# Chunk 0's second products on half rows, with the two PSUM banks exchanged between the halves

## The chip, the cores and the metric

The kernel runs on one core of one Trainium2 chip. Times are device microseconds of one execution; lower is better. Besides the timed runs there is one profiled execution, whose trace is read here. In the trace PE is the tensor engine (its matmuls; PEld its weight loads), DVE the vector engine, ACT ScalarE, POOL GpSimd, and SP the engine that issues most DMAs.

## The reference

`x` is (4, 4096, 192), `weight_gen` (4, 4096, 8, 7), `w_in` (192, 2048), `w_out` (2048, 192).

```
w = softmax(weight_gen, axis=-1)                 # 7 taps for each of 8 heads
att[b,s,h,:] = sum_k w[b,s,h,k] * x[b, s-6+k, h*24:(h+1)*24]    # zeros before the start
h = att.reshape(16384, 192) @ w_in               # float64 weights in memory
g = max(0.01 * h, h)
out = g @ w_out                                  # (16384, 192) float32
```

## The kernel before, in words

**Tiling.** The 16384 tokens are 32 chunks of 512 (`NCH`, `TOK`). The 2048 inner features are 16 blocks of 128 (`NF`), taken two at a time in 8 steps a chunk (`NQ`). Step q of the whole run belongs to chunk q // 8. In each step `mm1` computes `hp[2q]` and `hp[2q+1]` (128 features x 512 tokens each, one PSUM bank each): the first products. It works on half rows: the 192 inputs are three pairs of 64, and of every pair of matmuls one uses the upper and one the lower 64 rows of the array (`HALVES`), so the two run side by side. ScalarE applies the leaky ReLU, and the second products (`g` times a block of `w_out`) are summed over the 16 blocks in PSUM.

**Chunks 1 to 31** use f16 numbers split in an upper and a lower part (`wi_h`, `wi_l`, `g_h`, `g_l`). Their second products too use half rows: in one pass the upper rows write one bank and the lower rows another, and in a later pass they exchange. Two row groups must not write one bank at a time, so a nop on SP (`tell`, line 626) waits for the last matmul before the exchange, and the first one after it waits for the nop.

**Chunk 0** uses f32, because the scales of the f16 split are not known yet: the weights' maxima are being collected while chunk 0 is computed. An f32 matmul shows as two records in the trace, each streaming its columns twice. Its second products are in `mm2_whole` (line 649): for each block n four matmuls of 128 x 128 by 192 columns, on all 128 rows, into two banks `po0[0]` and `po0[1]`, each holding two row blocks of 128 tokens. `evacuate_whole` (line 662) copies `po0[0]` out on ScalarE and `po0[1]` on VectorE; the sums of chunk 1 (`new_sums`) take the same banks afterwards, and the first pair of `mm2_first` writes both.

**Order.** Each engine runs its instructions in the order written. The order of the first part is the string `START` (lines 55 to 62), one letter an action: `r` ScalarE reads a weight block's two words (`rnd`, then `mag`; lines 140, 141), `W` VectorE widens and adds them into `bits` (lines 151, 156), `m` takes the block's maximum (line 184), `f` is a step of first products with its two leaks on ScalarE, `e` is `mm2_whole` for one block, `p` and `q` are steps of the next chunks' convolution on GpSimd, `T` (`first_tokens`, line 419) copies the transposed tokens of chunk 0 from PSUM. `1`, `2`, `3` are the chain of the scales: two transposes of `both` on the PE (line 214), a matmul with `ones` (line 222), then the powers of two on VectorE (lines 191 to 228). `v`, `h`, `l` scale a block and split it into halves (VectorE line 241, ScalarE 249, VectorE 253); `H` and `L` (lines 258, 264) do the same without the copy in PSUM. `M N E B D C V y Y X R` prepare chunk 1's tokens.

The weight blocks come in the order of `order` (lines 722 to 725), (q, IN) for the first and (q, OUT) for the second products; the DMAs on SP, the reads and all later stages follow it. Tiles `rnd` and `mag` have three buffers each, `hp` four banks, `g` six.

From step 8 on `step(q)` (line 795) writes the order: first products, leak and cast of each `hp` (lines 567, 582) with VectorE's subtraction for `g_l` (line 585), the second products. In step 8 (`WHOLE * NQ`) it runs `mm2_whole` for the last two blocks of chunk 0 (`HOLD`) and `evacuate_whole`; `mm2_first` of chunk 1 starts in step 10. In chunk 1 every step also converts one weight block (`HL`) until all are done.

Of the kernel before, what the change touches and what calls it, by code (L numbers as in the profile page):

```python
# [8 lines left out]
F32 = mybir.dt.float32  # L9
F32R = mybir.dt.float32r  # L10
U32 = mybir.dt.uint32
I32 = mybir.dt.int32
F16 = mybir.dt.float16
AF = mybir.ActivationFunctionType
ALU = mybir.AluOpType
# [22 lines left out]

WHOLE = 1

HOLD = 2

TURNS = {1: (2, 3)}

G0 = 20
# [7 lines left out]
HEAT = 11  # L53

START = (
    "ZASgdgdtgdtgdrtgdtagdtgdWrttbT"
    "Wprmf"
    "WmrprfpWmrWpmrf"
    "WpmrWmreeeeWpmrWmrWpmrf"
    "WmrpsfWmrpWmreeeeWmrppppMNEBDCVWmfWmmf"  # L60
    "ee1yYXe2e3RvvhhllevvhhllevvhhllfvvhhllqqHL"
)


# [1 line left out]
def conv_attention_moe_kernel(  # L66
# [66 lines left out]
    NW = NB * P  # L133
    vals = {}

    def read_words(key):
        w = words.pop(key).rearrange("p a b w -> p (a b) w")
        rnd = raw.tile([P, NW], U32, tag="rnd", name="rnd", bufs=3)
        mag = raw.tile([P, NW], F32, tag="mag", name="mag", bufs=3)
        nc.scalar.activation(out=rnd, in_=w[:, :, 0], func=AF.Copy, scale=2.0 ** -29)  # L140
        nc.scalar.activation(  # L141
            out=mag, in_=w[:, :, 1].bitcast(F32), func=AF.Prelu, scale=REBIAS, alpha=SIGN
        )
        vals[key] = rnd, mag.bitcast(U32)

    def widen(key, add=False):

# [27 lines left out]
    most = const.tile([P, 2, NQ], F32, name="most")  # L175
    both = const.tile([P, 2], F32, name="both")
    scale = const.tile([P, 2, 2], I32, name="scale")[:, :, 0]
    back = const.tile([P, 2, 2], I32, name="back")[:, :, 0]
    undo = const.tile([P, 1], F32, name="undo")
    ones = const.tile([1, P], F32, name="ones")  # L180

# [26 lines left out]
    def weight_scales(i):  # L208

        if i == 0:  # L210
            nc.vector.tensor_reduce(out=both, in_=most, axis=AX.X, op=ALU.max)
            chain["t"] = spare()
            for k in range(2):
                nc.tensor.transpose(
                    out=chain["t"][0:1, k * P:(k + 1) * P], in_=both[:, k:k + 1], identity=ident
                )
        elif i == 1:
            row = chain.pop("t")[0:1, 0:2 * P].rearrange("p (k t) -> p k t", k=2)
            top = const.tile([1, 2], F32, name="top")
            nc.vector.tensor_reduce(out=top, in_=row, axis=AX.X, op=ALU.max)  # L220
            chain["b"] = spare()
            nc.tensor.matmul(out=chain["b"][:, 0:2], lhsT=ones, rhs=top, start=True, stop=True)  # L222
        else:
            e = spare()[:, 0:2].bitcast(I32)
            exponents(chain.pop("b")[:, 0:2], e)
            powers(e, scale, back)
            b = back.bitcast(F32)
            nc.vector.tensor_scalar(
                out=undo, in0=b[:, 0:1], scalar1=b[:, 1:2], scalar2=1.0 / DOWN,
                op0=ALU.mult, op1=ALU.mult,  # L230
            )

    def scale_of(key):
        return scale.bitcast(F32)[:, key[1]:key[1] + 1]
# [181 lines left out]
                skip_group_check=True,  # L416
            )

    def first_tokens():

        new_xx(0)
        lo, hi = HALVES
        x = xx[0].rearrange("p k i b t -> p (k i b t)").rearrange("p (n t) -> p n t", t=2 * P)
        a, b, c = (t[:, 0:2 * P] for t in sums)
        act, dve = nc.scalar.copy, nc.vector.tensor_copy
        act(out=x[:, 1], in_=a)  # L428
        dve(x[:, 2], b)
        softmax_exp(0, SECOND)  # L430
        act(out=x[:, 5], in_=c)
        dve(x[lo, 3], b[hi])
        act(out=x[lo, 0], in_=a[hi])
        dve(x[hi, 4], b[lo])
        act(out=x[hi, 0], in_=a[lo])
        dve(x[hi, 3], c[lo])
        act(out=x[lo, 4], in_=c[hi])

    def first_rows(b):

# [4 lines left out]

    FIRSTS = (
        (0, 0, 0), (1, 1, 0), (0, 2, 0), (1, 0, 1), (0, 1, 1), (1, 2, 1),
        (0, 1, 0), (1, 0, 0), (0, 0, 1), (1, 2, 0), (1, 1, 1), (0, 2, 1),
    )

    def mm1_first():
# [194 lines left out]
        for n in ns:  # L646
            del g_h[n], g_l[n]

    def mm2_whole(ns):

        for n in ns:
            f = n % NF
            for j in range(J):
                nc.tensor.matmul(  # L654
                    out=po0[j // 2][:, j % 2 * D:(j % 2 + 1) * D],
                    lhsT=g_h[n][:, POS[j] * P:(POS[j] + 1) * P], rhs=value((f // 2, OUT))[:, f % 2],
                    start=(f == 0 and j % 2 == 0), stop=(f == NF - 1 and j % 2 == 1),
                    skip_group_check=True,
                )
            del g_h[n]  # L660

    def evacuate_whole(c):

# [55 lines left out]
                    eng = nc.sync  # L719
                eng.dma_start(out=out_rows[:, r + j, :], in_=ot)  # L720

    order = [(0, IN), (1, IN), (2, IN), (0, OUT)]
    for q in range(3, NQ):
        order += [(q, IN), (q - 2, OUT)]
    order += [(NQ - 2, OUT), (NQ - 1, OUT)]
    done = dict.fromkeys("rwomvhl", 0)
    stages = dict(
# [22 lines left out]
    with tc.manual_schedule():  # L750
# [27 lines left out]
                else:  # L778
                    n -= 1

        pending = []

        def firsts(q):

# [10 lines left out]
        def step(q):  # L795

            c, i = divmod(q, NQ)
            if i == 0 and c in sm_q:
                load_weights(sm_q[c])
                load_rows(sm_q[c])  # L800
            if i == 1 and c in sm_q:
                softmax_max(sm_q[c])
                softmax_sub(sm_q[c], nc.gpsimd)
            begun, told = pending.pop() if pending else (None, None)
            mm1(q)
            leak(2 * q)
            if begun:
                mm2_second(begun, told)
                if begun[-1] % NF == NF - 1:
                    evacuate(begun[-1] // NF)  # L810
            if q == NP - 1:
                leak(2 * q + 1)
                split_g(2 * q, nc.vector)
            else:
                split_g(2 * q)
                if c + 1 < NCH and i == TURNS.get(c, (1, 3))[1] + 1:
                    squares(c + 1, 1)
                leak(2 * q + 1)
            split_g(2 * q + 1)
            if q == WHOLE * NQ:  # L820
                mm2_whole(range(2 * q - HOLD, 2 * q))
                evacuate_whole(c - 1)
            elif firsts(q):
                ns = firsts(q)
                pending.append((ns, tell(mm2_first(ns))))
            if c == WHOLE:
                for what in "HL":
                    if done[what.lower()] < len(order):
                        prepare(what)
            if i == 0:  # L830
                feed(c + 1, 2 * K)
            if c + 1 < NCH:
                first, turned = TURNS.get(c, (1, 3))
                if i == first:
                    scale_tokens(c + 1)
                if i == first + 1:
                    split_h(c + 1)
                    split_l(c + 1, nc.gpsimd)
                if i == turned:
                    squares(c + 1, 0)  # L840
                if i == turned + 1:
                    put_squares(c + 1)
                if i == turned + 2:
                    get_squares(c + 1)
                if i >= first:
                    feed(c + 2, 1 if c == WHOLE and i == first else 3)
            finish_softmax(c, i)
# [24 lines left out]
                    out=t, lhsT=zeros[:, 0:P], rhs=zeros, start=True, stop=True  # L872
                )

        n, added, ended = 0, 0, 0
        for what in START.replace(" ", ""):
            if what in stages:
                prepare(what)
# [31 lines left out]
                add_transposed(added)  # L910
                added += 1
            elif what == "T":
                first_tokens()
            elif what in "123":
                weight_scales("123".index(what))
            elif what == "B":
                scale_tokens(1)
            elif what == "M":
                softmax_max(1)
            elif what == "N":  # L920
                softmax_sub(1, nc.gpsimd)
            elif what == "E":
                softmax_exp(1)
            elif what == "D":
                m = spare()[:, 0:R * H].unsqueeze(2)
                sm[1] = win.tile([P, R * H, 1], F32, tag="sm", name="sm")
                nc.vector.tensor_reduce(out=m, in_=grouped(1, ALL), axis=AX.X, op=ALU.add)
                nc.vector.tensor_scalar_add(out=m, in0=m, scalar1=1e-9)
                nc.vector.reciprocal(out=sm[1], in_=m)
                softmax_div(1, nc.gpsimd)  # L930
            elif what == "q":
                feed(2, 1)
            elif what == "C":
                split_h(1)
            elif what == "V":
                split_l(1, nc.gpsimd)
            elif what in "yY":
                squares(1, "yY".index(what))
            elif what == "X":
                put_squares(1)  # L940
            elif what == "R":
                get_squares(1)
            elif what == "f":
                mm1(n) if n else mm1_first()
                leak_out(2 * n)
                leak_out(2 * n + 1)
                n += 1
            elif what == "e":
                mm2_whole([ended])
                ended += 1  # L950
            else:
                raise ValueError(what)
        for n in range(n, NP):
# [36 lines left out]
```

## Time and profile before

| what | value |
|---|---|
| median of 3 runs | 1029.55 us (1029.2 to 1030.83) |
| profiled execution | 1029.38 us, span 1027.6 us |
| PE busy | 1021.4 us, 99% of the span |
| ACT busy | 661.9 us, 64% |
| DVE busy | 570.8 us, 56% |
| POOL busy | 802.6 us, 78% |
| chunk 0's second products (line 654) | 128 records, 22.3 us of matmuls |
| chunk 0's first products (lines 458, 561) | 108 records in f32 |

The span is the time from the first to the last instruction; the execution's own time is 1.78 us longer. Busy shares are means over stages with different limits; the change is in the first 62 us.

### The profile page before, as it was taken

How to read it: one execution, taken by the hardware profiler on the slowest of the kernel's cores; microseconds unless marked ns; L12 is line 12 of the kernel's file. 1: busy time of each engine (PE TensorE's matmuls, PEld its weight loads, DVE VectorE, ACT ScalarE, POOL GpSimd, SP SyncE). 2: the span in 40 equal slices, each digit the busy share in tenths (PEclk: the TensorE clock that was granted, in tenths of full speed). 3: DMA queues.
4: the chain of work that ended last, by engine and by line, in shares of the span. 5: the costliest groups of instructions: out<-in, count | busy, mean ns of one | idle time of the engine just before them, and what ended most of it. 6: DMA issues, size and time to landing. Idle time of an engine off the chain costs nothing.

```text
span 1027.6 us, 30264 instructions
## 1 busy us (share of the span) xinstructions
PE 1021.4 (99%) x12821; PEld 906.9 (88%) x12821; DVE 570.8 (56%) x1033; ACT 661.9 (64%) x1264; POOL 802.6 (78%) x514
## 2 busy tenths in 40 slices
PE   8999999999999999999999999999999999999998
PEld 7778888988889898898988999899998988989897
DVE  8996545554545555455555455545456554555443
ACT  6586666666657666666666666666566666666664
POOL 7989798777897777887777987778987779987600
PEclk9999999999999999999999999999999999999999
DMA  9521312303232132322213123032321323120120
GB/s 256 166 91 48 126 48 71 117 28 116 63 110 64 44 99 63 118 55 63 95 48 126 48 65 119 26 122 63 97 78 40 103 63 115 58 64 33 48 63 17
DMA packets 42662, 83.08 MB, mean 81 GB/s; under 512 B 4511, under 2 KB 36127, under 8 KB 40734
## 3 DMA queue, kind: packets, MB, share of 16 engines
q1 hardware_dynamic: 42382, 81.05, 25.9%
q8 instruction: 100, 1.64, 0.7%
q14 instruction: 36, 0.29, 0.1%
q10 hardware_dynamic: 144, 0.10, 0.0%
HBM read 56.36 MB, written 24.77 MB: 79 GB/s over the span
## 4 chain that ended last, share of the span: by engine, by line
PE 99%; DMA 1%; SPq 0%; DVE 0%; ACT 0%; issue 0%; ACTq 0%
PE hp L561 52%; PE po L614 44%; PE po L654 2%; DMA wi_raw<-in_moe_w_in_dram 0%; PE hp L458 0%; DMA wt<-in_weight_gen_dram 0%; SPq L127 0%; SPq L283 0%; ACT mag L141 0%; DVE oe L715 0%; DVE wt L318 0%; ACT rnd L140 0%; DVE mx L315 0%; PE spares L222 0%; ACT xw L428 0%
## 5 line engine op out<-in xcount | busy, mean ns | idle before, releaser
L585 DVE TENSOR_TENSOR gl<-hp,gh 128x512 f16<-128x512 f32 x496 | 338.2, 688 | 379.8 <-ACT gh L582 376.3
L614 PE MATMUL po<-wo,gh 64*128 64x384 f16 (+1 forms) x4096 | 539.4, 318 | 0.0
L614 PE MATMUL po<-wo,gl 64*128 64x192 f16 x3968 | 519.6, 243 | 0.0
L561 PE MATMUL hp<-xx,wi_h 64*128 64x512 f16 x2976 | 501.7, 376 | 0.0
L567 ACT ACTIVATE hp<-hp 128x512 f32<-128x512 f32 x496 | 292.3, 589 | 269.9 <-PE hp L561 269.9
L614 PEld LDWEIGHTS <-gh 64*128 64x128 f16 x4096 | 375.7, 94 | 12.5
L561 PE MATMUL hp<-xx,wi_l 64*128 64x512 f16 x1488 | 381.5, 376 | 0.0
L614 PEld LDWEIGHTS <-gl 64*128 64x128 f16 x3968 | 369.0, 94 | 10.2 <-DVE gl L585 0.2
L363 POOL TENSOR_TENSOR acc<-acc,tmp 128x768 f32<-128x768 f32 x186 | 336.7, 1810 | 14.6
L582 ACT CAST gh<-hp 128x512 f16<-128x512 f32 x495 | 290.7, 587 | 16.1 <-PE po L614 1.5
L359 POOL TENSOR_TENSOR tmp<-xt,wt 128x768 f32<-128x768 f32 x186 | 287.7, 1547 | 10.0
L561 PEld LDWEIGHTS <-wi_h 64*128 64x128 f16 x2976 | 255.4, 94 | 45.4 <-issue 1.1
L561 PEld LDWEIGHTS <-wi_l 64*128 64x128 f16 x1488 | 139.3, 94 | 33.1
L502 POOL TENSOR_TENSOR acc<-acc,xu 128x768 f32<-128x768 f32 x30 | 44.1, 1470 | 137.7 <-DVE xu L201 137.7
L697 DVE SCALAR_TENSOR_TENSOR ot<-po,xr,ot 128x192 f32<-128x192 f32 x120 | 41.7, 410 | 50.6 <-ACT ot L693 50.6
L521 DVE STREAM_TRANSPOSE sq<-split 128x384 f16<-128x384 f16 x124 | 63.9, 554 | 8.7 <-POOL split L512 8.2
L508 ACT CAST split<-acc 128x768 f16<-128x768 f32 x31 | 25.8, 832 | 51.1 <-POOL acc L502 48.9
L512 POOL TENSOR_TENSOR split<-acc,split 128x768 f16<-128x768 f32 x31 | 50.9, 1643 | 1.0 <-ACT split L508 0.9
L359 POOL TENSOR_TENSOR acc<-xt,wt 128x768 f32<-128x768 f32 x31 | 48.1, 1553 | 1.2 <-ACT wt L323 1.2
L693 ACT ACTIVATE ot<-po,xr 128x192 f32<-128x192 f32 x120 | 40.7, 422 | 0.7
L485 DVE TENSOR_REDUCE xm<-acc 128x4 f32<-128x768 f32 x30 | 28.3, 943 | 0.3 <-POOL acc L363 0.3
L654 PEld LDWEIGHTS po<-bits,g 128*128 128x128 f32 x128 | 20.6, 190 | 2.7 <-DVE bits L156 1.5
(94 smaller groups left out, 291.6 us busy)
## 6 DMA issues: line engine op xcount, KB each, us to landing
xx<-far SPq DMA_DIRECT2D x124, 192.0 KB, 3.8
xt<-in_x_dram SPq DMA_DIRECT2D x14, 1344.0 KB, 5.7
far<-sq SPq DMA_DIRECT2D x31, 384.0 KB, 2.3
out_dram<-ot SPq DMA_DIRECT2D x62, 192.0 KB, 1.9
wt<-in_weight_gen_dram SPq DMA_DIRECT2D x15, 224.0 KB, 2.5
wi_raw<-in_moe_w_in_dram SPq DMA_DIRECT2D x16, 192.0 KB, 6.5
wo_raw<-in_moe_w_out_dram SPq DMA_DIRECT2D x8, 384.0 KB, 8.4
xt<-in_x_dram SPq DMA_DIRECT2D x2, 384.0 KB, 4.0
```

Source lines behind the costliest of these rows:

```text
L359: eng.tensor_tensor(out=out, in0=tap(c, k), in1=wk, op=ALU.mult)
L363: eng.tensor_tensor(out=acc, in0=acc, in1=out, op=ALU.add)
L502: nc.gpsimd.tensor_tensor(out=att[c], in0=att[c], in1=up.bitcast(F32).to_broadcast([P, J, D]), op=ALU.mult)
L512: eng.tensor_tensor(out=l, in0=att.pop(c), in1=h, op=ALU.subtract)
L521: nc.vector.transpose(out=sq[c][:, v, i], in_=src[:, v])
L561: nc.tensor.matmul(out=hp[2 * q + u], lhsT=w[s], rhs=r[u], start=(m == 0), stop=(m == len(passes) - 1),)
L567: return nc.scalar.activation(out=hp[n], in_=hp[n], func=AF.Prelu, alpha=0.01, scale=DOWN).ins
L582: nc.scalar.copy(out=h, in_=t)
L585: nc.vector.tensor_tensor(out=l, in0=t, in1=h, op=ALU.subtract)
L614: ins = nc.tensor.matmul(out=po[j][:, 0:b - a], lhsT=g[n][s, j * P:(j + 1) * P], rhs=wo[s, f, a:b], start=(f == 0 and i < HALF and m == 0) ...
L654: nc.tensor.matmul(out=po0[j // 2][:, j % 2 * D:(j % 2 + 1) * D], lhsT=g_h[n][:, POS[j] * P:(POS[j] + 1) * P], rhs=value((f // 2, OUT))[:, ...
L697: nc.vector.scalar_tensor_tensor(out=ot[:, j], in0=po[k * HALF + j][:, 0:D], scalar=rx[j], in1=ot[:, j], op0=ALU.mult, op1=ALU.add,)
```

## The change

Chunk 0's second products go from `mm2_whole` to `whole_rows`: each block's products on the upper 64 rows of the array go into one bank and those on the lower 64 rows into the other, side by side; `(` is this first half for one block. `|` (`turn_rows`) puts a nop on ScalarE that waits for the last such matmul, and exchanges the banks; `)` is the second half, whose first matmul waits for the nop. In most steps the PE now does `))((` and then `f`. The last two blocks' second halves and the copies out of `po0` move from step 8 to step 9, and step 8 gets the weight instructions `hhllHL` instead, which no longer stand in `START`.

A second-products block now stands one place sooner in `order`. In `first_tokens` the read of the second weight block no longer stands ahead of the copies but between them, and the matmuls of the first step are reordered to the copies. The scales' inverse goes to PSUM first; `undo` is computed later (`u`).

```diff
-    "ZASgdgdtgdtgdrtgdtagdtgdWrttbT"
+    "ZASgdgdtgdtgdrtgdtagdtgdWttbT"
     "Wprmf"
-    "WmrprfpWmrWpmrf"
-    "WpmrWmreeeeWpmrWmrWpmrf"
-    "WmrpsfWmrpWmreeeeWmrppppMNEBDCVWmfWmmf"
-    "ee1yYXe2e3RvvhhllevvhhllevvhhllfvvhhllqqHL"
+    "Wrpmf"
+    "((WrpmWrmr|f"
+    "))((WprmWrmrWpmr|f"
+    "))((WpmrWpmrWmr|f"
+    "))((spWmrWrmWmpppppM|NEfBDCV"
+    "))((WmWmm|f"
+    "))((1((yYX2|3vvhhlluRf"
+    "))))((vvhhllvvhhllqqvv|"
...
-            powers(e, scale, back)
...
+            chain["d"] = spares[0][:, NW:NW + 2].bitcast(I32)
+            powers(e, scale, chain["d"])
...
         softmax_exp(0, SECOND)
+        read_rnd(key)
+        dve(x[lo, 3], b[hi])
         act(out=x[:, 5], in_=c)
-        dve(x[lo, 3], b[hi])
+        dve(x[hi, 4], b[lo])
+        read_mag(key)
         act(out=x[lo, 0], in_=a[hi])
-        dve(x[hi, 4], b[lo])
-        act(out=x[hi, 0], in_=a[lo])
         dve(x[hi, 3], c[lo])
         act(out=x[lo, 4], in_=c[hi])
+        act(out=x[hi, 0], in_=a[lo])
...
+    def turn_rows():
+
+        told = nc.scalar.nop().ins
+        tc.add_manual_dep(told, last[0].name, after, reason="rows to leave")
+        gate.append(told)
+        turned[0] ^= 1
+
+    def whole_rows(n):
+
+        f = n % NF
+        for i in range(HALF):
+            for u, s in enumerate(HALVES):
+                k = u ^ turned[0]
+                ins = nc.tensor.matmul(
+                    out=po0[k][:, i * D:(i + 1) * D],
+                    lhsT=g_h[n][s, POS[k * HALF + i] * P:(POS[k * HALF + i] + 1) * P],
+                    rhs=value((f // 2, OUT))[s, f % 2],
...
+                if gate:
+                    tc.add_manual_dep(ins, gate.pop().name, after, reason="rows left")
+        last[0] = ins
...
-    order = [(0, IN), (1, IN), (2, IN), (0, OUT)]
-    for q in range(3, NQ):
-        order += [(q, IN), (q - 2, OUT)]
+    order = [(0, IN), (1, IN)]
+    for q in range(2, NQ):
+        order += [(q - 2, OUT), (q, IN)]
...
             if q == WHOLE * NQ:
-                mm2_whole(range(2 * q - HOLD, 2 * q))
+                for what in "hhllHL":
+                    prepare(what)
+            elif q == WHOLE * NQ + 1:
+                for n in range(ended[0], NF):
+                    whole_second(n)
                 evacuate_whole(c - 1)
```

## Rows read from the trace of the kernel before

**Rows 1.** The page: engines' busy time, and the clock in 40 slices.

```profile
PE 1021.4 (99%) x12821; PEld 906.9 (88%) x12821; DVE 570.8 (56%) x1033; ACT 661.9 (64%) x1264; POOL 802.6 (78%) x514
...
PEclk9999999999999999999999999999999999999999
```

**Rows 2.** The chain of waits in order of time: start us, us, what ran.

```profile
19.84 5.40 PE po L654 x32
25.24 5.35 PE hp L561 x24
...
41.34 2.80 PE po L654 x16
...
50.06 4.72 PE hp L561 x30
54.78 2.80 PE po L654 x16
```

**Rows 3.** Timeline of PE, narrow windows: start, us, instruction, records merged.

```profile
17.50 1.05 PE L561 MATMUL hp<-xw,bits 64*128 64x512 f32 x4
18.79 1.05 PE L561 MATMUL hp<-xw,bits 64*128 64x512 f32 x4
20.04 0.49 PE L654 MATMUL po<-bits,g 128*128 128x192 f32 x2
24.91 0.33 PE L654 MATMUL po<-bits,g 128*128 128x192 f32 x1
...
43.97 0.38 PE L214 MATMUL spares<-ident,both 128*1 128x128 f32 x2
44.19 1.47 PE L654 MATMUL po<-bits,g 128*128 128x192 f32 x8
...
61.41 0.32 PE L614 MATMUL po<-wo,gh 64*128 64x384 f16 x1
```

**Rows 4.** Weight loads by form: count, busy us, mean ns, idle before.

```profile
L654 PEld LDWEIGHTS po<-bits,g 128*128 128x128 f32 x128 | 20.6, 190 | 2.7 <-DVE bits L156 1.5 <-DVE spares L151 0.8 <-ACT g L572 0.4
L561 PEld LDWEIGHTS hp<-xw,bits 64*128 64x128 f32 x84 | 8.2, 187 | 8.4 <-issue 8.4
```

**Rows 5.** Timelines of PE and ACT where the first products start.

```profile
10.44 0.60 PE L412 MATMUL ta<-ident,parts 128*128 128x128 f32 x4
11.80 2.89 PE L458 MATMUL hp<-xw,bits 64*128 64x256 f32 x24 [0.55 <-ACT xw L428]
...
11.39 0.36 ACT L428 COPY xw<-ta 128x256 f32<-128x256 f32 x1
```

**Rows 6.** Timeline of ACT: the reads numbered 10 and 11.

```profile
24.49 0.56 ACT L140 ACTIVATE rnd<-wo_raw 128x384 uint32<-128x384 uint32 x1 [1.34 <-DVE most L184]
...
26.09 0.56 ACT L140 ACTIVATE rnd<-wi_raw 128x384 uint32<-128x384 uint32 x1 [0.59 <-DVE most L184]
26.56 0.54 ACT L141 ACTIVATE mag<-wi_raw 128x384 f32<-128x384 f32 x1
27.68 0.56 ACT L140 ACTIVATE rnd<-wo_raw 128x384 uint32<-128x384 uint32 x1 [0.57 <-DMA wo_raw<-in_moe_w_out_dram]
```

**Rows 7.** Timeline of ACT in steps 8 and 9.

```profile
55.13 0.48 ACT L249 CAST wi_h<-spares 128x384 f16<-128x384 f32 x1 [0.16 <-DVE spares L241]
...
56.03 0.62 ACT L258 ACTIVATE wi_h<-bits,scale 128x384 f16<-128x384 f32 x1
56.55 0.59 ACT L567 ACTIVATE hp<-hp 128x512 f32<-128x512 f32 x1
...
58.76 0.48 ACT L671 COPY ot<-po 128x384 f32<-128x384 f32 x1
```

**Rows 8.** Timeline of DVE in step 8.

```profile
58.89 0.69 DVE L585 TENSOR_TENSOR gl<-hp,gh 128x512 f16<-128x512 f32 x1 [0.41 <-ACT gh L582]
59.50 0.55 DVE L669 COPY ot<-po 128x384 f32<-128x384 f32 x1
```

**Rows 9.** Line 264 (`L`): count, ns min/median/max, first and last start.

```profile
L264 DVE SCALAR_TENSOR_TENSOR wo<-bits,scale,wo x5: 603/1047/2232, 60.0 to 81.1; 128x384 f16<-128x384 f32 x5
```

More of the change, by code (lines that the diff above doesn't have):

```diff
@@ L39 @@
 WHOLE = 1
-HOLD = 2
 TURNS = {1: (2, 3)}
@@ L55 @@
 START = (
-    "ZASgdgdtgdtgdrtgdtagdtgdWrttbT"
+    "ZASgdgdtgdtgdrtgdtagdtgdWttbT"
     "Wprmf"
-    "WmrprfpWmrWpmrf"
-    "WpmrWmreeeeWpmrWmrWpmrf"
-    "WmrpsfWmrpWmreeeeWmrppppMNEBDCVWmfWmmf"
-    "ee1yYXe2e3RvvhhllevvhhllevvhhllfvvhhllqqHL"
+    "Wrpmf"
+    "((WrpmWrmr|f"
+    "))((WprmWrmrWpmr|f"
+    "))((WpmrWpmrWmr|f"
+    "))((spWmrWmrWmpppppM|NEfBDCV"
+    "))((WmWmm|f"
+    "))((1((yYX2|3vvhhlluRf"
+    "))))((vvhhllvvhhllqqvv|"
 )
@@ L134, in conv_attention_moe_kernel, with read_rnd, read_mag @@
     vals = {}
-    def read_words(key):
+    def read_rnd(key):
+        w = words[key].rearrange("p a b w -> p (a b) w")
+        rnd = raw.tile([P, NW], U32, tag="rnd", name="rnd", bufs=3)
+        nc.scalar.activation(out=rnd, in_=w[:, :, 0], func=AF.Copy, scale=2.0 ** -29)
+        vals[key] = rnd
+    def read_mag(key):
         w = words.pop(key).rearrange("p a b w -> p (a b) w")
-        rnd = raw.tile([P, NW], U32, tag="rnd", name="rnd", bufs=3)
         mag = raw.tile([P, NW], F32, tag="mag", name="mag", bufs=3)
-        nc.scalar.activation(out=rnd, in_=w[:, :, 0], func=AF.Copy, scale=2.0 ** -29)
         nc.scalar.activation(
@@ L143, in read_words @@
         )
-        vals[key] = rnd, mag.bitcast(U32)
+        vals[key] = vals[key], mag.bitcast(U32)
+    def read_words(key):
+        read_rnd(key)
+        read_mag(key)
     def widen(key, add=False):
@@ L177, in conv_attention_moe_kernel @@
     scale = const.tile([P, 2, 2], I32, name="scale")[:, :, 0]
-    back = const.tile([P, 2, 2], I32, name="back")[:, :, 0]
+    back = const.tile([P, 2, 2], F32, name="back")[:, :, 0]
     undo = const.tile([P, 1], F32, name="undo")
@@ L225, in weight_scales, with undo_scales @@
             exponents(chain.pop("b")[:, 0:2], e)
-            powers(e, scale, back)
[L227 to L231, printed above, removed]
+            chain["d"] = spares[0][:, NW:NW + 2].bitcast(I32)
+            powers(e, scale, chain["d"])
+    def undo_scales():
+        d = chain.pop("d").bitcast(F32)
+        nc.vector.tensor_copy(back, d)
+        nc.vector.tensor_scalar(
+            out=undo, in0=d[:, 0:1], scalar1=back[:, 1:2], scalar2=1.0 / DOWN,
+            op0=ALU.mult, op1=ALU.mult,
+        )
     def scale_of(key):
@@ L417, in add_transposed, with first_tokens @@
             )
-    def first_tokens():
+    def first_tokens(key):
         new_xx(0)
@@ L430, in first_tokens @@
         softmax_exp(0, SECOND)
+        read_rnd(key)
+        dve(x[lo, 3], b[hi])
         act(out=x[:, 5], in_=c)
-        dve(x[lo, 3], b[hi])
+        dve(x[hi, 4], b[lo])
+        read_mag(key)
         act(out=x[lo, 0], in_=a[hi])
-        dve(x[hi, 4], b[lo])
-        act(out=x[hi, 0], in_=a[lo])
         dve(x[hi, 3], c[lo])
         act(out=x[lo, 4], in_=c[hi])
+        act(out=x[hi, 0], in_=a[lo])
     def first_rows(b):
@@ L447, in conv_attention_moe_kernel @@
         (0, 0, 0), (1, 1, 0), (0, 2, 0), (1, 0, 1), (0, 1, 1), (1, 2, 1),
-        (0, 1, 0), (1, 0, 0), (0, 0, 1), (1, 2, 0), (1, 1, 1), (0, 2, 1),
+        (0, 0, 1), (1, 2, 0), (0, 1, 0), (1, 1, 1), (0, 2, 1), (1, 0, 0),
     )
@@ L647, in mm2_second, with whole_first, whole_second @@
             del g_h[n], g_l[n]
[L649 to L657, printed above, removed]
-                    skip_group_check=True,
-                )
-            del g_h[n]
+    turned, begun_in, last, gate = [0], {}, [None], []
+    def turn_rows():
[12 more added lines that the diff above has]
+                    rhs=value((f // 2, OUT))[s, f % 2],
+                    start=(f == 0 and i == 0 and n not in begun_in),
+                    stop=(f == NF - 1 and i == HALF - 1 and n in begun_in),
+                    skip_group_check=True,
+                ).ins
+                if gate:
+                    tc.add_manual_dep(ins, gate.pop().name, after, reason="rows left")
+        last[0] = ins
+    def whole_first(n):
+        whole_rows(n)
+        begun_in[n] = turned[0]
+    def whole_second(n):
+        assert begun_in[n] != turned[0]
+        whole_rows(n)
+        del g_h[n]
     def evacuate_whole(c):
@@ L779, in feed @@
                     n -= 1
-        pending = []
+        pending, begun0, ended = [], [0], [0]
         def firsts(q):
@@ L873, in heat @@
                 )
-        n, added, ended = 0, 0, 0
+        n, added = 0, 0
         for what in START.replace(" ", ""):
@@ L912, in conv_attention_moe_kernel @@
             elif what == "T":
-                first_tokens()
+                first_tokens(order[done["r"]])
+                done["r"] += 1
             elif what in "123":
                 weight_scales("123".index(what))
+            elif what == "u":
+                undo_scales()
             elif what == "B":
@@ L947, in conv_attention_moe_kernel @@
                 n += 1
-            elif what == "e":
-                mm2_whole([ended])
-                ended += 1
+            elif what == "(":
+                whole_first(begun0[0])
+                begun0[0] += 1
+            elif what == ")":
+                whole_second(ended[0])
+                ended[0] += 1
+            elif what == "|":
+                turn_rows()
             else:
```

## The prediction

> **What bounds the kernel now.** I read the page's engine shares first: the PE is busy 99% of the span, and the clock line shows the full level in every slice [rows 1]. The chain of waits, in order of time, says the same of the stretch that is changed: from 19.84 us on its pieces are PE runs one behind another [rows 2]. So a microsecond that the PE loses or gains in chunk 0 reaches the end as one. The profiled execution took 1029.38 us (span 1027.6 and 1.78 around it); the median of the runs is 1029.55, 0.17 above it. The sum is made against 1029.38.
>
> Inside the PE runs some time is no streaming. A pair of half-row matmuls of chunk 0's first products follows the last by 0.43 us (17.50 to 18.79 is three pairs), a whole-row record of the second products by 0.1625 us (20.04 to 24.91 is thirty) [rows 3]. So 24 records of first products are 12 x 0.43 = 5.16 us, and 32 records of second products 5.20. The run of first products between two whole-row runs takes 5.35, and the whole-row run 5.40 [rows 2]. Going to whole rows and back thus costs 0.20 + 0.19 = 0.4 us.
>
> **What the change removes.** There are four such trips: the runs from 19.84 and 30.59 (alike, one row shown), the one from 41.34 with the scales' chain in it, and the held products from 54.78 [rows 2]. The last is cheaper, since half rows in f16 follow it: 2.80 - 16 x 0.1625 = 0.20 and some 0.10 around it. Together 3 x 0.4 + 0.3 = 1.5 us. With half rows all through, the mode stays. Two matmuls of the chain still break it. The transposes of `both` take 0.22 us now, inside a whole-row run (43.97 to 44.19) [rows 3]; afterwards they stand among half rows and need a trip of their own, +0.4. The matmul with `ones` uses one row and breaks either mode: of the 8.72 us from 41.34 to 50.06, 48 x 0.1625 = 7.80 are products, 0.20 the entry and exit, 0.22 the transposes, so 0.50 is its price [rows 2, 3], and I leave it. Net: -1.1 us (bounds 0, if the exchange of banks breaks the stream as a trip does, and -1.5).
>
> **The streaming itself.** A pair of half-row matmuls does what one whole-row matmul did, so 128 records become 128 pairs. No f32 pair of 192 columns is in the trace. The nearest is the pair of 512 columns: 0.43 is 192/512 of which 0.161, against 0.1625. Weight loads for half rows take 187 ns, for whole rows 190 ns [rows 4], and the latter pass at 0.1625. I take 0; the ends are -0.2 us (128 x 0.0015) and +3.1 us, where every pair waited for a full load (128 x 0.0245).
>
> **The start.** The first products wait for ScalarE's copy of 11.39 and start 0.41 later [rows 5]. ScalarE stood before that copy in the second weight block's read. With that read behind the copy, the copy starts at about 10.9, when the transposes of 10.44 are through, and the products at 11.3; the first weight block ends no sooner. But the block's two reads (0.5 us each) now stand between the copies, so the third and the last of the six pairs wait for theirs, some 0.25 us together. I take -0.24 us; ends 0 and -0.49.
>
> **What is late next, first place: the gate.** "|" is a nop on ScalarE; it waits for the PE's `((`, and the PE's `))` waits for it. Behind it on ScalarE stand the next step's leaks, which need a later matmul anyway. Ahead of it stand the reads of weight words, which wait for their loads. By PE time: the first two steps' first products end at 14.49 - 0.24 = 14.25 and, 2.58 later, 16.83; then `((` (eight pairs, 1.3 us) 18.13, third 20.71, `))((` 23.31, fourth 25.89. There the PE needs the nop that stands behind the reads numbered 8 to 11. Before, the 10th and 11th began at 24.49 and 26.09 behind gaps, the 11th ending at 27.10 [rows 6]; the profile puts those gaps to the vector engine, but that read's buffers were long free and the next gap, equally spaced, is a load's. The blocks' order changes, their number up to the 11th doesn't. So the PE would wait until 27.1: 1.25 us. Two things shorten it: the 11th is now a second-products block, one issue in place of two, and the delay before the 10th (1.34 us idle) may not come back at that place. Ends 0 and 1.25, taken 0.9, nearer the row. The first gate, at 20.71, has the 7th read ending near 20.7 (the second step's leaks end about 17.9, and three reads of 0.9 follow); I count 0 for it, 0.25 is in the range. The later gates have their reads done about a microsecond before.
>
> PE time goes on: `))((` 29.4, fifth 32.0, sixth 37.2, seventh 42.35, `))((` 44.95, transposes 45.55, `((` 46.85, `ones` 47.35, eighth 49.93, `))))((` 53.83, and step 8's first products end at t = 55.78 (1.95 us of f16). Chunk 1's tokens and the first weight halves are needed later than now, and are no new wait.
>
> **Second place: chunk 0's banks.** The copies that empty `po0` move from step 8 to step 9, behind step 9's four leak and cast instructions; six more weight instructions of ScalarE and VectorE ("hhllHL") go into step 8 ahead of them. Chunk 1's second products at step 10 write those two banks with their first pair. In PE time they are ready after step 9's first products, the last `))` and step 10's: t + 1.95 + 1.30 + 1.95 = t + 5.2, or 60.98 (now 61.41 [rows 3]). ScalarE's line by its own rows [rows 7]: from t + 0.2 four leaks and casts at 2.21 (56.55 to 58.76), two `h` at 0.90 (55.13 to 56.03), two `H` at 0.52, again 2.21: the copy starts at t + 6.55 and ends at t + 7.03. VectorE's copy is queued behind the subtraction that needs the last cast (t + 6.7): 0.61 from that subtraction's start to the copy's, 0.55 the copy [rows 8], so t + 7.9. The PE waits 7.9 - 5.2 = 2.7 us. Before, both copies stood ahead of this work and nothing waited.
>
> Two `L` instructions of VectorE also stand in that line. Five of the eight took 0.60 to 2.23 us, median 1.05 [rows 9]. At 0.60 VectorE reaches the last subtraction some 0.4 us ahead of its cast; two at 1.05 add 0.9, so 0.5 beyond that slack, and the wait would be 3.2. I take 3.1. Ends: 1.9, where only ScalarE's copy counted (t + 7.03, and a little), and 5.6, where both took 2.23.
>
> On these `L` the Trainium skill speaks ("SBUF — State Buffer", Who interferes with whom): a vector instruction with two SBUF inputs waits out a whole GpSimd instruction that reads SBUF. The spread in [rows 9] agrees with it; by it the wait at the banks comes to its upper end where both `L` meet a fresh GpSimd instruction.
>
> **Sum.** -1.1 (trips) - 0.24 (start) + 0.9 (gate) + 3.1 (banks) = +2.7 us: 1029.38 + 2.7 = 1032.1 us.
>
> **Rivals.**
> *The banks come free in time.* Place: step 10's first pair; it decides for the other side if both copies are through by t + 5.2. For it: ScalarE idles just before t and could catch up if its queue were shorter. Against it: eight leaks and casts and four weight instructions between t and the copy are 6.35 us by rows. Then -1.34 + 0.9 = 1028.9 us, without the gate 1028.0: not slower, but inside 0.2%. Chance 0.20.
> *The gate doesn't hold the PE, the banks do.* Loads come 1.2 us sooner. 1029.38 - 1.34 + 3.1 = 1031.1. Chance 0.17.
> *The pairs wait for their weights.* +3.1 us on top: 1035.2 us. Against it, whole-row loads of 190 ns pass at 0.1625 [rows 3, 4]. Chance 0.05.
> The Trainium skill ("TensorE: Matmul & The Clock Gate", LDWEIGHTS) gives 128 columns / 1.2 = 107 ns a load whatever the rows; two groups loading by turns would by that estimate need 214 ns a pair, some 6.6 us more. No run so far shows it.
> *The change doesn't do what it says:* the exchange breaks the stream as a trip does, and nothing is saved: 1033.2. Chance 0.05. The granted clock could also fall in the wait at the banks (it is at its upper level, 2.4 GHz, all through [rows 1], and no wait is that long now); the same side, 1033 to 1035, chance 0.03.
> *More is saved than I see,* beyond 0.2%: 0.07.
> The forecast itself: 0.43.
>
> **How the numbers follow.** 0.2% is 2.06 us, about what a measurement of this kernel tells from no change: slower means above 1031.6. The forecast's own range is 1031.0 to 1033.6 and lies above that bound in some 5 of 6 cases (0.36); the three slower rivals add 0.13, the gate's rival 0.05 with longer `L`: 0.54. Faster is 0.08, within 0.2% 0.38. From 1028.0 to 1034.0 leaves out the faster case, part of the first rival and the dearest ones, some 0.18.
>
> **What would show it.** Right: second products in half-row records, no step of 0.26 us between the kinds of run but at the scales' chain, pairs 0.163 apart; first products from 11.3; a gap of up to a microsecond behind the fourth first products, put to ScalarE; a gap near 3 us ahead of the first f16 second products, put to the copy out of `po`. Wrong: no gap there, or VectorE's copy done before step 10's first products end; pairs at 0.187 or more; a lower granted clock.

## The result, and the profile after

| what | before | after |
|---|---|---|
| median | 1029.50 us (6 runs, 1029.17 to 1030.83) | 1035.99 us (6 runs, 1034.97 to 1037.42) |
| ratio | | 1.0062, 95% interval 1.0051 to 1.0072 |
| profiled execution | 1029.38 us, span 1027.6 | 1037.42 us, span 1035.6 |

The change costs 6.5 us (5.3 to 7.4 by the interval). I had forecast +2.7 and a range up to 1034.0: the sign was right, the size was not. Three of the six executions after list a mean granted clock of 0.996 (1036.01 to 1037.42 us) and three 0.998 (1034.97 to 1035.98 us); the profiled one is the slowest of the six, 1.4 us above their median.

The page of the kernel after, where [rows 1] showed a full clock in every slice: one slice, the third (52 to 78 us), is lower.

```profile
PE 1025.3 (99%) x12949; PEld 910.8 (88%) x12949; DVE 569.6 (55%) x1034; ACT 661.7 (64%) x1264; POOL 802.5 (77%) x514
...
PEclk9989999999999999999999999999999999999999
```

The chain of waits after (start us, us, what ran). Where [rows 2] had runs of 5.40 and 5.35 on the PE, there are now 2.60 and 2.57, one right behind the other. At 57 us the chain leaves the PE for ScalarE, and from 59.45 to 66.76 it runs on VectorE:

```profile
33.30 2.60 PE po L679 x32
35.90 2.57 PE hp L576 x12
...
60.60 0.47 DVE wi_l L268
61.07 1.68 DVE wo L279
62.75 1.81 DVE wi_l L279
64.56 0.53 DVE mx L330
65.09 1.20 DVE gl L600 x2
66.29 0.47 DVE ot L707
...
66.81 3.70 PE po L629 x15
70.51 3.10 PE hp L576 x18
```

The PE's timeline after (in brackets: idle before, and who ended it). To be read against [rows 3] and [rows 5]: the start, the gate at 27.86, and the two waits for the banks.

```profile
11.82 0.60 PE L427 MATMUL ta<-ident,parts 128*128 128x128 f32 x4
12.80 2.86 PE L473 MATMUL hp<-xw,bits 64*128 64x256 f32 x23 [0.16 <-DVE bits L166]
...
24.60 0.59 PE L576 MATMUL hp<-xw,bits 64*128 64x512 f32 x1
27.86 2.87 PE L679 MATMUL po<-bits,g 64*128 64x192 f32 x32 [0.35 <-ACTq L668]
...
61.82 0.59 PE L576 MATMUL hp<-xx,wi_l 64*128 64x512 f16 x2
63.84 0.32 PE L629 MATMUL po<-wo,gh 64*128 64x384 f16 x1 [1.43 <-ACT ot L709]
66.81 0.48 PE L629 MATMUL po<-wo,gh 64*128 64x384 f16 x1 [2.65 <-DVE ot L707]
```

The stretches after by engine (busy us and count of PE, PEld, DVE, ACT, POOL; then the granted clock, DMA share, GB/s):

```profile
62.00:64.00 2.00, 0.57 (x4) 0.09 (x1) 2.00 (x2) 1.97 (x5) 1.92 (x2) 1.00 0.00 0
64.00:66.00 2.00, 0.16 (x1) 0.00 (x0) 2.00 (x4) 1.94 (x5) 1.92 (x2) 0.90 0.27 98
66.00:68.00 2.00, 1.20 (x11) 1.13 (x12) 2.00 (x4) 1.03 (x2) 1.16 (x2) 0.50 0.18 65
68.00:70.00 2.00, 2.00 (x20) 1.90 (x18) 2.00 (x4) 0.00 (x0) 0.00 (x0) 0.50 0.09 34
70.00:72.00 2.00, 2.00 (x15) 1.53 (x12) 0.67 (x4) 0.00 (x0) 1.08 (x1) 0.50 0.00 0
72.00:74.00 2.00, 2.00 (x24) 1.60 (x22) 0.00 (x0) 0.50 (x1) 1.89 (x2) 0.89 0.01 4
```

The reader is to see that the PE did almost nothing from 62.04 (61.82 and two records of 0.11) to 66.81, and that the clock is then granted at 0.50, the lower level of 1.2 GHz, until past 72 us, although the PE is fully busy from 68 on.

**The balance of the profiled execution.** Chunk 1's second products began at 61.41 before [rows 3] and run from 66.81 after: 5.40 us. The span grew by 8.0, so 2.6 us lie behind that point. The chain shows where: from the start of these second products to the end of the next step's first products it is 6.80 us now (66.81 to 73.61), and it was 4.22 (61.41 to 65.63), so 2.58 of the 2.6 are lost in the stretch at the lower clock. The row of before that begins at that end:

```profile
65.63 2.86 PE po L614 x46
```

The 5.40 are: start +1.00 (first products from 12.80 instead of 11.80), the stretch from there to the banks -0.37 (49.24 us to 62.04, before 49.61), and the wait at the banks 4.77. In the -0.37 the gate stands with +0.69 (24.60 to 27.86 is 3.26, where such a run takes 2.57), so the trips gave -1.06.

The start's +1.00 is not the change's: the tokens' second load landed later in this execution. VectorE's row of before and, in the second fence, of after:

```profile
6.39 2.35 DVE L382 TENSOR_TENSOR parts<-xt,po 128x480 f32<-128x480 f32 x4 [0.24 <-DMA xt<-in_x_dram]
```

```profile
7.78 2.35 DVE L397 TENSOR_TENSOR parts<-xt,po 128x480 f32<-128x480 f32 x4 [1.59 <-DMA xt<-in_x_dram]
```

That is 1.39 late; from the last transposes to the first products it is 0.98 (11.82 to 12.80) where it was 1.36 [rows 5]. So the start itself gained 0.39. In the profiles of the experiments with this code the same row begins between 6.29 and 7.38: it varies from execution to execution. Without it the terms are -0.39 - 1.06 + 0.69 + 4.77 + 2.6 = +6.6, and the medians differ by 6.5. That is closer than it need be: the 2.6 is from an execution at 0.996, and half of the six list 0.998.

### The profile page after: what moved, and what is told of

Its sections match the earlier page's. It is cut to its first block, busy times and chain, and to the rows that moved or that the text cites. A ratio compares the mean times of both kernels' runs of the same rounds, so it can differ in the third digit from the quotient of the medians.

```text
span 1035.6 us, 30528 instructions
## 1 busy us (share of the span) xinstructions
PE 1025.3 (99%) x12949; PEld 910.8 (88%) x12949; DVE 569.6 (55%) x1034; ACT 661.7 (64%) x1264; POOL 802.5 (77%) x514
## 4 chain that ended last, share of the span: by engine, by line
PE 96%; DMA 2%; DVE 1%; ACT 0%; SPq 0%; issue 0%; ACTq 0%
PE hp L576 50%; PE po L629 44%; PE po L679 2%; DMA wi_raw<-in_moe_w_in_dram 1%; DMA wo_raw<-in_moe_w_out_dram 1%; DMA wt<-in_weight_gen_dram 1%; DVE gl L600 0%; DVE wi_l L279 0%; DVE wo L279 0%; ACT gh L597 0%; ACT hp L582 0%; DVE mx L330 0%; SPq L129 0%; DVE ot L707 0%; DVE wi_l L268 0%
## 5 line engine op out<-in xcount | busy, mean ns | idle before, releaser
L679 PEld LDWEIGHTS po<-bits,g 64*128 64x128 f32 x256 | 22.1, 187 | 3.6 <-issue 1.6
```

The lines of the kernel that those rows point to most:

```text
L679: ins = nc.tensor.matmul(out=po0[k][:, i * D:(i + 1) * D], lhsT=g_h[n][s, POS[k * HALF + i] * P:(POS[k * HALF + i] + 1) * P], rhs=value((f ...
```

## The experiments

Each was timed beside the kernel before on the same chip (its medians there: 1029.98 with e1 to e4, 1030.41 with e5 to e7, 1029.9 with e8). The profiles can be put in one table: where chunk 1's second products run from, against 61.41 before, and the span against 1027.6.

| kernel | second products of chunk 1 | span | median's ratio (interval) |
|---|---|---|---|
| after | +5.40 | +8.0 | 1.0062 (1.0051 to 1.0072) |
| e1 | +1.93 | +1.8 | 1.0014 (1.0005 to 1.0023) |
| e2 | +1.34 | +1.4 | 1.0004 (0.9995 to 1.0012) |
| e3 | +5.01 | +5.0 | 1.0048 (1.0035 to 1.0061) |
| e5 | -1.08 | -0.7 | 0.9991 (0.9982 to 1.0) |
| e6 | +4.84 | +4.7 | 1.0021 (1.0012 to 1.003) |
| e7 | +3.41 | +3.4 | 1.0019 (1.001 to 1.0028) |
| e8 (e5 again) | -0.87 | -0.4 | 0.9991 (0.9982 to 1.0) |

In each but one the two columns agree within half a microsecond: what is lost or won is settled by 67 us. The exception is the changed kernel, by 2.6 us, and among these traces it alone shows the lower clock there. A single profile can lie well off its kernel's median (e6: its execution took 1034.21, the median is 1032.7).

**e1: step 8's weight instructions behind the copies.**

```diff
-                for what in "hhllHL":
+                for what in "hhll":
...
-                for what in "HL":
+                for what in "HL" * {8: 0, 10: 2, 11: 2}.get(q, 1):
```

> The changed kernel with the two H and two L weight instructions of step 8 moved behind the copies out of po0 (steps 9 to 11); the two h and two l stay in step 8. Theory A (the loss is the PE's wait for the copies out of po0, 4.1 us in the trace of the changed kernel, and the lower clock behind it, about 2.9 us): VectorE's copy ends some 6.9 us after step 8's first products instead of 9.9, the PE waits about 1.6 us, the granted clock stays at its upper level, and the time is 1036.0 - 2.5 - 2.9 = 1030.6 us (1029.9 to 1031.3). Theory B (the half-row products, their exchange or the weights' new order cost the time, and the wait only takes up what was lost before): 1033.5 or more. Theory C (the clock falls because of the half-row work, not because of the wait): the wait shrinks, the clock falls all the same, about 1033.5.

Measured: 1031.34 us, +1.4 us (0.5 to 2.4). PE's waits at the banks are 0.42 for ScalarE's copy and 0.49 for VectorE's, 1.60 in all (61.74 to 63.34), instead of 4.77, and the clock is full throughout; all ten executions list 0.999 or 1.0. So the bulk of the loss was these instructions' place in the queue, and with a wait of 1.6 us the clock stays. Of the terms, -0.39 - 1.06 + 0.62 (its gate) + 1.60 = +0.8, in the lower part of the interval.

**e2: e1, and the second halves and the copies back in step 8.**

```diff
             if q == WHOLE * NQ:
-                for what in "hhll":
-                    prepare(what)
-            elif q == WHOLE * NQ + 1:
                 for n in range(ended[0], NF):
                     whole_second(n)
                 evacuate_whole(c - 1)
+                for what in "hhll":
+                    prepare(what)
```

> As the first run, and the last two second halves and the copies out of po0 go back to step 8, ahead of its h and l. Theory A: the copies end some 3.7 us after step 8's first products, before the PE needs the banks at 5.2; a wait of at most 0.5 us is left (for the casts of step 9), the clock stays, and what the half rows save shows: 1036.0 - 3.8 - 2.9 = 1029.3 us (1028.3 to 1029.9). Theory B: 1033 or more. Theory C: a fall of the clock without a wait, about 1032.

Measured: 1030.4 us, +0.4 us (-0.5 to +1.2), above the 1028.3 to 1029.9 that I had expected. No wait at a bank is left in its trace, but the PE stands at the gate, twice (timeline of PE of this kernel):

```profile
27.91 2.87 PE L679 MATMUL po<-bits,g 64*128 64x192 f32 x32 [1.35 <-ACTq L668]
...
33.72 2.54 PE L679 MATMUL po<-bits,g 64*128 64x192 f32 x28 [0.37 <-ACTq L668]
```

That left the question whether the gate is all that keeps the half rows from paying: e5.

**e3: the changed kernel with the PE kept busy in the wait.** Twenty matmuls on zeros, into a bank that nothing reads, stand ahead of step 10's second products; they add nothing to the output.

```diff
+                if q == WHOLE * NQ + 2:
+                    t = ps_o.tile([P, TOK], F32, tag="o3", name="busy")
+                    for m in range(20):
+                        nc.tensor.matmul(
+                            out=t, lhsT=zeros[:, 0:P], rhs=zeros, start=True, stop=True
+                        )
```

> The changed kernel with 20 extra matmuls of zeros (128 x 128 by 512 columns, 0.216 us each, 4.3 us in all) into a bank that is free, placed in the PE's order where it waits for po0. Theory A: the wait for the copies is filled and not shortened, the clock stays at its upper level, and the time falls by what the lower clock cost: 1036.0 - 2.9 = 1033.1 us (1032.5 to 1033.8). Theory C: the clock falls all the same, 1036.

Measured: 1034.68 us, +4.9 us (3.6 to 6.3), above the 1032.5 to 1033.8 that I had expected. That is 1.4 us less than the changed kernel, with *more* work on the PE, but uncertain by 1.7, so the medians alone do not show a gain. The granted clock does show the effect: all four executions list 1.0, where the changed kernel's six list 0.996 or 0.998. The stretches of this kernel, columns as above, and its row of PE:

```profile
64.00:66.00 2.00, 2.00 (x10) 1.65 (x10) 2.00 (x5) 1.94 (x5) 2.00 (x2) 1.00 0.26 93
66.00:68.00 2.00, 2.00 (x29) 1.25 (x29) 2.00 (x4) 0.34 (x1) 0.40 (x1) 1.00 0.27 98
68.00:70.00 2.00, 2.00 (x26) 1.04 (x22) 1.90 (x6) 0.00 (x0) 0.00 (x0) 1.00 0.00 0
```

```profile
61.65 4.83 PE L870 MATMUL busy<-zeros 128*128 128x512 f32 x20
66.42 0.34 PE L629 MATMUL po<-wo,gh 64*128 64x384 f16 x2
```

The clock is full where it was 0.50, and nothing is lost behind 66.42 (+5.01 and +5.0 in the table). The filling overshoots: VectorE's copy ended at 65.95, the second products start 0.47 later. 1.4 + 0.47 = 1.9 of the 2.6 us are so accounted for; the rest is less than the uncertainty of 1.7.

**e4: the start alone.** The kernel before with the new `first_tokens` (second block's read between the copies).

```diff
         softmax_exp(0, SECOND)
+        read_rnd(key)
+        dve(x[lo, 3], b[hi])
         act(out=x[:, 5], in_=c)
...
+        read_mag(key)
         act(out=x[lo, 0], in_=a[hi])
```

> The kernel before with the change's first_tokens alone: the second input block's read between the copies of the tokens, the first step's matmuls reordered. Theory A: the first products start some 0.4 us sooner and lose 0.2 of it among the copies: 1029.5 - 0.25 = 1029.25 us (1029.0 to 1029.5). If the reads among the copies cost more than the earlier start gives: 1029.8 or more.

Measured: 1029.79 us against 1029.98, ratio 0.9999 (0.999 to 1.0007), where I had expected 1029.0 to 1029.5 against 1029.5. In this kernel's own trace the first products follow the row of the tokens' second load by 4.98 us, before by 5.41. For the time it is inconclusive: a gain of 0.39 us as read in the trace, and none at all, both lie in the interval.

**e5: e2 with the gate one or two reads sooner.** In steps 3 to 5 the nop stands ahead of a read instead of behind it.

```diff
-    "((WrpmWrmr|f"
-    "))((WprmWrmrWpmr|f"
-    "))((WpmrWpmrWmr|f"
+    "((WrpmWr|mrf"
+    "))((WprmWr|mrWpmrf"
+    "))((Wpmr|WpmrWmrf"
```

> The kernel of e2 (copies out in step 8, no wait at a bank) with the gate for the second weights' blocks put one or two reads earlier on ScalarE in steps 3 to 5, so that ScalarE opens it before the read that came last in e2. Theory A: what is left of e2 above the kernel before is TensorE standing at the gate (1.35 and 0.37 us in its rows, about 2.3 with the pipeline's drain and fill); with the gate opened a read of 0.5 to 1.4 us sooner, no first products wait there by over 0.2 us, and the time falls by 1 to 2 us against e2's ratio of 1.0004, to about 0.999 of the kernel before (1028.5 to 1029.5 on a chip where that takes 1030). Rival B: the reads behind the gate are now late themselves (weights' blocks or the later quantisation hold TensorE instead): the ratio stays at 1.0004 or rises, and the new wait stands in the rows of TensorE in steps 3 to 6.

Measured: 1029.52 us, ratio 0.9991 (0.9982 to 1.0): 1.3 us under e2, uncertain by 1.3. The trace has no wait at the gate and none at the banks, and this is the first version with half rows whose median lies under that of the kernel before. What is late next stands in its chain of waits: it leaves the PE at 53.41 and goes back over the tokens' round trip to VectorE, whose work on the weights' blocks (three instructions a block, 1.5 us) follows without a gap.

```profile
24.10 0.56 DVE bits L166
24.66 0.46 DVE most L194
25.11 0.48 DVE spares L161
...
44.82 2.90 DMA far<-sq
...
49.14 4.22 DMA xx<-far
53.41 2.06 PE hp L576 x17
```

The PE loses only 0.25 us to it there (step 8's first four f16 records take 0.71 until the next, 52.92 to 53.63; in the changed kernel 0.46), but it is the next bound.

**e6: the changed kernel with only the two `L` moved.** The `H` of step 8 stay ahead of the copies.

```diff
-                for what in "hhllHL":
+                for what in "hhllH":
...
-                for what in "HL":
+                for what in {8: "H", 9: "LLHL"}.get(q, "HL"):
```

> The changed kernel with only the two low-half operations (the ones with two SBUF inputs) of step 8 moved on VectorE behind the copies out of the banks; the two high-half operations stay ahead. Theory A: the long part of the wait for the bank was these two operations, 1.76 and 1.89 us behind GpSimd's; without them VectorE's copy ends at 7.9 us after step 8's first products (9.9 in the changed kernel), the wait is about 2.7 instead of 4.77 us, the granted clock then stays at its upper level, and the time is the kernel before's plus 1.5 to 2.2 us (ratio 1.0015 to 1.0021). Rival B: the clock falls after the shorter wait too: plus 4 to 4.5 us (1.004). Rival C: VectorE's copy is held by something else ahead of it (ScalarE's exchange of banks, late high halves): the wait stays over 4 us and the ratio at 1.006.

Measured: 1032.7 us, +2.2 us (1.2 to 3.1), 4.2 us under the changed kernel. Timelines of PE and then of VectorE in this kernel:

```profile
56.71 0.60 PE L576 MATMUL hp<-xx,wi_h 64*128 64x512 f16 x3 [1.13 <-DMA xx<-far]
...
63.42 0.59 PE L576 MATMUL hp<-xx,wi_l 64*128 64x512 f16 x2
65.44 0.32 PE L629 MATMUL po<-wo,gh 64*128 64x384 f16 x1 [1.43 <-ACT ot L709]
66.25 0.32 PE L629 MATMUL po<-wo,gh 64*128 64x384 f16 x1 [0.49 <-DVE ot L707]
```

```profile
65.04 0.69 DVE L600 TENSOR_TENSOR gl<-hp,gh 128x512 f16<-128x512 f32 x1 [0.41 <-ACT gh L597]
65.65 0.55 DVE L707 COPY ot<-po 128x384 f32<-128x384 f32 x1
66.11 0.77 DVE L279 SCALAR_TENSOR_TENSOR wo<-bits,scale,wo 128x384 f16<-128x384 f32 x1
66.80 0.61 DVE L279 SCALAR_TENSOR_TENSOR wi_l<-bits,scale,wi_h 128x384 f16<-128x384 f32 x1
```

The copy ends at 66.20, 7.75 us after step 8's first products (58.45 here); the wait is 2.61 us (63.64 to 66.25), 2.16 less than with the `L` ahead; the clock stays full in this execution; and 2.16 + 2.6 = 4.8 stands against the 4.2 by which the medians differ (uncertain by 1.4). ScalarE's copy alone now ends the longer part of the wait. Behind the copy, with GpSimd nearly idle, the same two `L` take 0.77 and 0.61.

The clock did not stay full in every execution: five of the ten list 0.998, as three of the changed kernel's do (their median is 1032.86, that of the other five 1032.09). No execution of any other experiment, nor of the kernel before beside them, lists less than 0.999. So with these instructions gone the lower clock comes in some executions and not in others. How long the PE stood in those five is not known, since the one kept trace is of an execution at 1.0.

**e7: e5 with whole rows.** Chunk 0's second products on all 128 rows, at the places of the second halves, so that there are no first halves and no gate; all else as in e5.

```diff
     def whole_second(n):
-        assert begun_in[n] != turned[0]
-        whole_rows(n)
+        f = n % NF
+        for j in range(J):
+            nc.tensor.matmul(
+                out=po0[j // 2][:, j % 2 * D:(j % 2 + 1) * D],
+                lhsT=g_h[n][:, POS[j] * P:(POS[j] + 1) * P], rhs=value((f // 2, OUT))[:, f % 2],
...
```

> The kernel of e5 with chunk 0's second products on whole rows again: all else (copies, gate, blocks' places, start) as in e5. It tells what the half rows alone are worth. Theory A: each switch between the two array shapes costs 0.4 us, whole rows put seven of them back (plus the ones at the transposes), and the pairs' pitch is the same: e5 plus 1.1 to 2.8 us (ratio higher by 0.0011 to 0.0027). Rival B: the switches cost nothing that the end sees, or half-row pairs are slower than their share: the same as e5 within 0.5 us, or faster.

Measured: 1032.47 us, ratio 1.0019 against e5's 0.9991: 2.9 us (uncertain by 1.3), where I had expected 1.1 to 2.8. The chain of waits of this kernel has the trips, to be laid beside 2.60 and 2.57 above:

```profile
41.30 2.78 PE hp L576 x12
44.07 2.80 PE po L675 x16
```

2.78 + 2.80 against 2.57 + 2.60 is 0.41 us for a trip there and back. The 2.9 us are not seven such trips alone, though, for the PE also stands where e5 has first halves to do (timeline of PE):

```profile
18.93 2.85 PE L576 MATMUL hp<-xw,bits 64*128 64x512 f32 x12 [0.90 <-ACT g L587]
...
47.59 0.38 PE L232 MATMUL spares<-top,ones 1*128 1x2 f32 x2 [0.51 <-DVE top L230]
```

From its first products to chunk 1's second products this kernel takes 52.46 us (12.36 to 64.82) and e5 48.90 (11.43 to 60.33). Of the 3.56 between them 1.27 stand ahead of 18.93: the run from 15.08 is 2.58 long and ends at 17.66. So at most 2.3 are left for the trips, and what e7 measures is the half rows together with the order that they allow.

**e8: e5 once more.**

> The kernel of e5 once more, to see whether its gain stands: e5 gave a ratio of 0.9991 with an interval that reaches 1.0. Theory A: the trips' saving (1.1 us) and the start's (0.2 to 0.4) are real and nothing is paid for them here, so the ratio comes out between 0.998 and 0.9995, with no wait of TensorE at the gate or the banks. Rival B: the gain was the spread of single executions, whose loads land up to 1.4 us apart: 1.0 or above.

Measured: 1029.0 us against 1029.9, again 0.9991 (0.9982 to 1.0), with no wait at the gate or the banks. Two runs of 11 executions give the same -0.9 us, so I take the gain as real, though each interval alone just reaches 1.0.

## Why the prediction was wrong, step by step

**Trips: right.** Forecast -1.1, the trace -1.06; 0.41 a trip (e7) against 0.4. The transposes of the scales' chain cost 0.51 among half rows (0.31, and 1.50 instead of 1.30 for the eight pairs behind them), 0.22 before: +0.29, where +0.4 was counted.

**Streaming: right.** 32 half-row records, 16 pairs, take 2.60 us: 0.1625 a pair. The rival of loads by turns is refuted. The weight loads after, by form (count, busy us, mean ns, idle before):

```profile
L679 PEld LDWEIGHTS po<-bits,g 64*128 64x128 f32 x256 | 22.1, 187 | 3.6 <-issue 1.6 <-ACTq L668 1.5
```

Each takes 187 ns, and a pair of them passes in 0.1625 us, so the two groups' loads overlap. The estimate of 214 ns a pair that I drew from the Trainium skill ("TensorE: Matmul & The Clock Gate", LDWEIGHTS) doesn't hold for this: that section of the Trainium skill prices one load, and that the two halves load by turns was my addition.

**Start: right in the trace** (-0.39 against -0.24), too small to show in the time (e4).

**Gate: right in place, and in size partly by luck** (0.69 against 0.9). It holds for a load (ScalarE, after): the 10th and 11th of the reads stand behind the weights' DMAs, as forecast.

```profile
26.27 0.57 ACT L141 ACTIVATE rnd<-wi_raw 128x384 uint32<-128x384 uint32 x1 [0.77 <-DMA wi_raw<-in_moe_w_in_dram]
...
27.73 0.56 ACT L141 ACTIVATE rnd<-wo_raw 128x384 uint32<-128x384 uint32 x1 [0.45 <-DMA wo_raw<-in_moe_w_out_dram]
```

I had the gate open at the end of the 11th read, 27.10 (which is 1.21 behind 25.89, not 1.25). In the trace it lets the PE go 0.13 us after that read's start (27.73 to 27.86) and does not wait for its end. But the read starts 1.6 us later than the 26.09 that I took, and after the late start the PE comes to the gate at 27.17 and not at 25.89. These errors nearly cancel. In the four other traces with the same code ahead of the gate the PE again goes 0.12 to 0.13 us after that read's start, and what it loses is 0.62 (e1), 0.21 (e3), 2.0 (e6) and 2.1 (e2, at two places), so my upper end of 1.25 was too low. What I did not see either is that the gate need not stand behind that read at all; e5 gets 1.3 us (uncertain by 1.3) from moving it.

**Banks: the first step that failed, by size.** The mechanism, its place and the order of the two copies were as written. ScalarE's copy began 6.45 us after the end of step 8's first products (63.30 - 56.85), forecast 6.55. VectorE's ended at 9.9 (66.76 - 56.85), forecast 7.9 and with the `L` some 0.4 more. I put two `L` at their median of 1.05 and took off a slack of 0.4 us. They took 1.68 and 1.81 in the chain, and behind them stood a reduction of 0.53 that I had not counted. e6 shows that this was the error: without them the copy ends at 7.75. So the `L` were worth 2.16 us at the banks, not 0.4, and the wait was 4.77, not 3.1. It lies inside the ends that I gave (1.9 to 5.6).

The median was the wrong row to take, since the cause of the spread in [rows 9] was in hand. GpSimd after:

```profile
60.52 1.81 POOL L378 TENSOR_TENSOR acc<-acc,tmp 128x768 f32<-128x768 f32 x1
62.41 1.74 POOL L374 TENSOR_TENSOR tmp<-xt,wt 128x768 f32<-128x768 f32 x1
64.23 2.00 POOL L378 TENSOR_TENSOR acc<-acc,tmp 128x768 f32<-128x768 f32 x1
```

The first `L` starts at 61.07 in the chain and ends at 62.75, 0.42 behind the end of GpSimd's first (62.33). By then GpSimd's next has begun (62.41), and the second `L` ends at 64.56, 0.41 behind the end of that one. GpSimd runs nearly without a pause here (1.92 of every 2 us in the windows), so two `L` in a row at this place meet it, and the second pays for almost a whole GpSimd instruction. An `L` that comes late in one pays little: in e1 one starts at 63.20, 0.24 us ahead of such an end (63.44), and takes 0.66. That is the rule of the Trainium skill ("SBUF — State Buffer", Who interferes with whom) that I had weighed and then priced by a median; the trace agrees with it, 1.68 and 1.81 here against 0.77 and 0.61 with GpSimd nearly idle (e6).

**The granted clock: the second step that failed, a term that the sum put at nothing.** I had it as a rival of chance 0.03 and should have tied it to the wait. It cost 2.6 us by the balance of the profiled execution, and it is what carried the result out of the range: without it the terms make +4.0, 1033.4 us. That it was the standing PE is shown by e3 (the same wait, the PE busy, the clock at 1.0 in all four executions) and by e1 (a wait of 1.6 us, 0.999 or more in all ten); e6 lies between (a wait of 2.6 us at full clock in its trace, 0.998 in five of ten executions). By my own upper end, a wait of 5.6 us, this rival was no accident but part of the case; it belonged on the long side of the banks' term.

Together: banks +1.7 over the forecast, clock +2.6, gate and start -0.4 under it: +2.7 becomes +6.6.

**The other rivals.** Banks free in time: true only when the copies go back to step 8 (e2, e5), and then the sign turns as that rival had it, 1029.0 to 1029.5. Tokens that are no new wait: true in the changed kernel's trace, but in e3 and e6, whose code is the same up to there, the PE stands 0.44 and 1.13 us for them, and in e5 they are the next bound.

## What to carry to other kernels

When an instruction is moved ahead of a copy that frees a bank, price it by what GpSimd runs at that moment, not by its mean, and look at what the PE does meanwhile: a wait of 4.8 us cost 7.4 in the trace here, and one of 2.6 cost 2.6 in the trace of e6, though half of that kernel's executions list a lower clock. A switch of the array's shape costs 0.41 us there and back in f32 and is worth removing, but only together with the places of the copies and of the gate that the new order needs (e5). A gate belongs ahead of the first instruction on its engine that waits for a load.

## What the runs showed of the hardware that I had not expected

The clock's return was slow: granted at 0.50 from about 66 to past 72 us, with the PE at work from 66.81 on. Filling the wait with matmuls that nobody needs kept the clock at 1.0 in all four executions, and the program was 1.4 us faster (e3, uncertain by 1.7). A nop behind a read on ScalarE let the PE go 0.12 to 0.13 us after the read's start, in five traces, and not at its end. VectorE's first use of the tokens' second load varies from 6.29 to 7.78 us between traces with this start, and the first products follow it by 4.97 to 5.17 us in each of them, so the load's landing goes straight into the time.
